# Loading two weight matrices by head, moving integer adds from GpSimd to VectorE, and reordering the first loads of a fused attention and feed-forward kernel

## The chip, the cores and the metric

The kernel runs on one core of a Trainium2 chip. The metric is device time in microseconds, from the median of several executions; lower is better. The engines named below are TensorE (PE in the profile; its weight loads are PEld), VectorE (DVE), ScalarE (ACT), GpSimd (POOL) and SyncE (SP), which issues all DMA transfers of this kernel. The core has 16 DMA engines.

## The reference

The inputs are q, k, v, a_re and a_im of shape (4, 8, 768, 48), that is batch, heads, time and width of a head, in float32. The weights w1 and w2 (384 x 1024), w3 (1024 x 1024) and w_out (1024 x 384) come in float64.

```python
mag = np.sqrt(a_re * a_re + a_im * a_im)
scale = np.minimum(mag, 0.999) / (mag + 1e-06)
a_re_n, a_im_n = (a_re * scale, a_im * scale)
for t in range(S):
    new_re = ar * S_re - ai * S_im          # ar, ai: row t of a_re_n, a_im_n
    new_im = ar * S_im + ai * S_re
    S_re, S_im = (new_re + k_t v_t^T, new_im)
    y[:, :, t] = q_t @ S_re
x = y.transpose(0, 2, 1, 3).reshape(B * S, H * D)
out = ((x @ w1) * (x @ w2)) @ w3 @ w_out
```

## The kernel before, in words

The host passes q, k and the gates with time last, v with the heads beside each other, and w3 transposed; the float64 weights are passed as they are.

The work is cut into eight units of 384 time steps, two to a batch. For each unit `gates(u)` computes the running product of the gates on ScalarE, VectorE and GpSimd (logarithm, exponential, arctangent, scans, sine) and scales q and k with it. `parts` splits its operations into three for unit 0 only. At its end copies from one place of the on-chip memory to another (line 563) lay the results out by head as KL and QL, and it requests unit u+2's gates. `scores` and `outputs` do the attention in three chunks of 128 steps. `ffn_ab` multiplies by w1 and w2 (line 636), and `ffn_out` by one matrix w3 @ w_out (line 646), which the kernel computes beforehand in `fuse` (line 713).

All weights are converted from float64 words to float32 in `convert`. A raw tile holds pairs of 32-bit words, 128 rows of up to 8 KB; three raw tiles rotate (pool `cv3`). ScalarE makes `low`, the rounded top bits of the low word (line 668), and `mag`, the square that finds tiny values (669). VectorE shifts and masks the high word (670, 672). An integer add puts `low` on it (673), and VectorE multiplies by the result of a comparison (674). `low` and `mag` have one buffer each, the converted tile two. There are 18 conversions: four of w_out (128 x 768 values each), eight of w3 and six of w1 and w2 (128 x 1024 each).

For w1 and w2 the rows are laid out as the attention delivers them: tile 0 holds the first 32 rows of heads 0 to 3, tile 1 those of heads 4 to 7, tile 2 the last 16 rows of all eight heads. Each tile is one transfer whose source has heads as its outermost dimension, then rows, then 8 KB of words.

The list `work` holds w_out's four conversions, then for each of eight columns of w3 a conversion and a `fuse`, then w1's and w2's six conversions. The main program calls them in turn and takes one step of unit 0's `gates` after each. Then the pools of the conversion are closed (line 760), and a pool `late` is opened in their place, which holds unit 1's q, k and results. After that a loop over the units mixes attention, feed-forward of the unit before, and steps of the next unit's gates.

A tile framework takes these calls as the order of precedence. A planner in it fixes, before the kernel runs, each engine's own order of instructions from dependencies, free buffers and its estimate of durations. On the chip every engine then works strictly in that order, SyncE's issues too. Each transfer waits on one of eight transfer semaphores that are used in turn, so at most eight transfers are on their way. A last branch computes everything in another way if the gates are out of bounds; it isn't taken with these inputs.

Of the kernel before, what the change touches and what calls it, by code (L numbers as in the profile page):

```python
# [10 lines left out]
FP = mybir.dt.float32  # L11
# [3 lines left out]
OP = mybir.AluOpType  # L15
# [300 lines left out]
def kernel(  # L316
# [37 lines left out]
    nc = tc.nc  # L354
    B, H, D, S = qt.shape
    P = 128
# [6 lines left out]
    KF = FF // P  # L363
# [3 lines left out]
    LO, HI = 32, D - 32  # L367
# [48 lines left out]
    def load_rows(dst, src, u):  # L416
        b, h = divmod(u, 2)
        for f in range(KD):
            nc.sync.dma_start(out=dst[:, f, 0:TT], in_=src[b, :, DG * f:DG * (f + 1), h * TT:(h + 1) * TT].rearrange(  # L419
                "h d s -> d h s"))  # L420

    def load_gates(u):
        g = g_t[u] = {}
        for n, src in (("re", art), ("im", ait)):
            g[n] = two.tile([P, KD, TT], FP, tag=n, name=n)
            load_rows(g[n], src, u)

    def load_qkv(u):
        b, h = divmod(u, 2)
        g = g_t[u]  # L430
        g["q"] = sides[u % 2].tile([P, KD, TT], FP, tag="q", name="q")
        g["k"] = sides[u % 2].tile([P, KD, TT + UC], FP, tag="k", name="k")
        load_rows(g["k"], kt, u)
        load_rows(g["q"], qt, u)

        vr = one.tile([P, UC, DM], FP, tag="vr", name="vr")
        nc.sync.dma_start(out=vr, in_=v[b, h * TT:(h + 1) * TT].rearrange("(c p) e -> p c e", p=C))
        g["vr"] = vr
# [217 lines left out]
    LOAD = 1024  # L656
    MIN_SQ = (1.125 * 2.0 ** -15) ** 2

    def convert(dst, src):
        r, m = dst.shape[1:]  # L660
        raw = cv3.tile([P, r, m, 2], I32, tag="raw", name="raw")
        nc.sync.dma_start(out=raw.rearrange("p r m w -> p r (m w)"), in_=src)
        lo, hi = raw[:, :, :, 0], raw[:, :, :, 1]
        low = cv1.tile([P, r, m], I32, tag="low", name="low")
        mag = cv1.tile([P, r, m], FP, tag="mag", name="mag")
        f = cv2.tile([P, r, m], FP, tag="cf", name="cf")
        b = f.bitcast(I32)
        nc.scalar.activation(out=low, in_=lo.bitcast(U32), func=AF.Copy, scale=2.0 ** -29)  # L668
        nc.scalar.activation(out=mag, in_=hi.bitcast(FP), func=AF.Square)
        nc.vector.tensor_scalar(out=b, in0=hi, scalar1=3, scalar2=0x3FFFFFFF, op0=OP.logical_shift_left,  # L670
                                op1=OP.bitwise_and)
        nc.vector.scalar_tensor_tensor(out=b, in0=hi, scalar=-0x40000000, in1=b, op0=OP.bitwise_and, op1=OP.bitwise_or)  # L672
        nc.gpsimd.tensor_tensor(out=b, in0=b, in1=low, op=OP.add)  # L673
        nc.vector.scalar_tensor_tensor(out=dst, in0=mag, scalar=MIN_SQ, in1=f, op0=OP.is_ge, op1=OP.mult)  # L674

    def load_weight(dst, src):
        if src.dtype == FP:
            nc.sync.dma_start(out=dst, in_=src)
        else:
            convert(dst, src)  # L680

    def words(src):
        return src if src.dtype == FP else src.bitcast(I32)

    def w12_work():

        got = []
        for d, w in ((w1s, w1), (w2s, w2)):
            hs = words(w).rearrange("(h e) m -> h e m", e=D)
            for f, src in enumerate((hs[0:4, 0:LO], hs[4:8, 0:LO], hs[:, LO:D])):  # L690
                got.append(lambda d=d, f=f, src=src: load_weight(d[:, f:f + 1], src))
        return got

    wo_s = one.tile([P, KF, DM], FP, tag="ab", name="wo_s")
    w3_t = {}

    def wo_work():
        src = words(wo).rearrange("(i p) m -> p i m", p=P)
        return [lambda i=i: load_weight(wo_s[:, i:i + 2], src[:, i:i + 2]) for i in range(0, KF, 2)]

    def w3_work(j):
        n = 1 if w3t.dtype == FP else 2
        src = words(w3t).rearrange("(i p) m -> p i m", p=P)[:, :, n * j * P:n * (j + 1) * P]

        def load():
            w3_t[j] = two.tile([P, KF, P], FP, tag="xT", name="w3s")
            load_weight(w3_t[j], src)
        return [load]

    def fuse(j):  # L710
# [34 lines left out]
    cv2 = conv.enter_context(tc.tile_pool(name="cv2", bufs=2))  # L745
    cv3 = conv.enter_context(tc.tile_pool(name="cv3", bufs=3))
    load_gates(0)
    load_qkv(0)
    work = wo_work()
    for j in range(KF):  # L750
        work += w3_work(j) + [lambda j=j: fuse(j)]
    work += w12_work()
    start = gates(0, True)
    load_gates(1)
    for i, f in enumerate(work):
        f()
        next(start, None)
    for _ in start:
        pass
    conv.close()  # L760
    sides[1] = fast.enter_context(tc.tile_pool(name="late", bufs=1))
    load_qkv(1)
# [63 lines left out]
```

## Time and profile before

| what | value |
|---|---|
| median of 3 runs | 746.97 us (745.07 to 749.74) |
| profiled execution | 749.98 us, span 748.2 us |
| TensorE busy | 587.1 us (78%) |
| VectorE busy | 354.0 us (47%) |
| ScalarE busy | 256.2 us (34%) |
| GpSimd busy | 147.9 us (20%) |
| moved by DMA | 65.76 MB, mean 88 GB/s |

Times in the profile are microseconds from the start of the span unless marked ns. A row of a group reads: line, engine, operation, output<-input, shapes, count, then busy time and mean ns of one, then the idle time before it and what ended it. A row of the waits reads: who <- for whom, total us, times, longest. A row of the timeline reads: start, length, engine, line, operation. "SPq" is SyncE's queue of issues. The DMA share is the mean busy share of the 16 DMA engines. TensorE's granted clock is given as a share of full speed.

### The profile page before, as it was taken

The numbers are of one execution on the slowest core, as the hardware profiler recorded it, in microseconds if no ns is written. First come the engines' busy times: TensorE is split into PE (matmuls) and PEld (weight loads), VectorE is DVE, ScalarE is ACT, GpSimd is POOL, SyncE is SP. The second block draws the span as 40 slices with busy tenths as digits, with TensorE's granted clock in tenths as the row PEclk, the third lists the DMA queues.
The fourth block names the chain that finished last, engine by engine and source line by source line (L and its number), as shares of the span: only waits on it lengthen the run. The fifth ranks groups of instructions, "written<-read, shape, count | busy, mean of one in ns | idle before, by whom it ended". The sixth has DMA issues, their size and how long they took to land.

```text
span 748.2 us, 8868 instructions
## 1 busy us (share of the span) xinstructions
PE 587.1 (78%) x3514; PEld 381.9 (51%) x3514; DVE 354.0 (47%) x491; ACT 256.2 (34%) x362; POOL 147.9 (20%) x131
## 2 busy tenths in 40 slices
PE   0028788038882489997998989999988998999997
PEld 0014465024451365674566646765675567567553
DVE  3889715334857457425811681178038713112110
ACT  6444531225464634315403540363046202100110
POOL 5474403414212141102101210131023000000000
PEclk9999998659997589999998999999989999999999
DMA  8755963452079670395301950097047005500001
GB/s 234 243 169 160 185 142 113 119 141 83 2 108 155 80 134 0 96 117 106 95 1 31 131 157 1 0 127 191 1 62 98 11 0 77 73 0 23 13 0 36
DMA packets 44563, 65.76 MB, mean 88 GB/s; under 512 B 3808, under 2 KB 42720, under 8 KB 43744
## 3 DMA queue, kind: packets, MB, share of 16 engines
q1 hardware_dynamic: 44512, 65.10, 43.5%
q8 instruction: 29, 0.48, 0.3%
q14 instruction: 22, 0.18, 0.1%
HBM read 41.42 MB, written 4.72 MB: 62 GB/s over the span
## 4 chain that ended last, share of the span: by engine, by line
PE 49%; DVE 20%; ACT 10%; DMA 8%; issue 7%; POOL 2%; SPq 2%; DVEq 0%; ACTq 0%; POOLq 0%
PE m L636 18%; PE o L646 16%; DMA raw<-in_w_dram 6%; PE sc L583 5%; DVE gZ L533 3%; PE kv L619 3%; DVE gA L508 3%; PE tp L578 2%; ACT gZ L469 2%; ACT gR L469 2%; POOL cf L673 2%; SPq L419 1%; PE f L713 1%; DVE cf L670 1%; ACT KT L579 1%
## 5 line engine op out<-in xcount | busy, mean ns | idle before, releaser
L636 PE MATMUL m<-xT,w1s 128*128 128x384 f32 x384 | 141.7, 506 | 20.6 <-ACT xT L614 12.7
L636 PE MATMUL m<-xT,w2s 128*128 128x384 f32 x384 | 136.0, 490 | 5.3 <-ACT a L640 2.9
L646 PE MATMUL o<-w3o,ab 128*128 128x384 f32 x384 | 129.5, 494 | 0.7 <-DVE ab L641 0.7
L636 PEld LDWEIGHTS m<-xT,w1s 128*128 128x128 f32 x384 | 73.4, 197 | 74.9 <-DVE ab L641 14.5
L636 PEld LDWEIGHTS m<-xT,w2s 128*128 128x128 f32 x384 | 73.0, 191 | 59.3 <-ACT a L640 6.0
L584 DVE COPY_PREDICATED A<-causal,sc 128x512 f32<-128x512 int32 x48 | 35.1, 738 | 140.3 <-PE sc L583 140.0
L646 PEld LDWEIGHTS o<-w3o,ab 128*128 128x128 f32 x384 | 72.5, 192 | 49.1 <-issue 2.1
L713 PE MATMUL f<-wo_s,w3s 128*128 128x384 f32 x128 | 50.3, 556 | 59.3 <-DVE w3s L674 59.3
L641 DVE TENSOR_TENSOR ab<-m,a 128x384 f32<-128x384 f32 x64 | 35.4, 552 | 96.1 <-PE m L636 93.1
L713 PEld LDWEIGHTS f<-wo_s,w3s 128*128 128x128 f32 x128 | 27.4, 218 | 81.4 <-DVE w3s L674 59.0
L640 ACT COPY a<-m 128x384 f32<-128x384 f32 x64 | 30.2, 474 | 110.3 <-PE m L636 110.2
L484 POOL TENSOR_TENSOR im<-im,gR 128x1152 f32<-128x1152 f32 (+1 forms) x10 | 20.7, 2075 | 199.4 <-ACT gR L469 194.7
L673 POOL TENSOR_TENSOR cf<-cf,low 128x1024 int32<-128x1024 int32 (+1 forms) x18 | 47.3, 2630 | 59.4 <-DVE cf L672 30.4
L583 PE MATMUL sc<-QL,KL 96*128 96x128 f32 x384 | 55.6, 309 | 0.0
L583 PEld LDWEIGHTS sc<-QL,KL 96*128 96x128 f32 x384 | 53.0, 221 | 3.0 <-issue 1.0
L579 ACT COPY KT<-tp 128x384 f32<-128x384 f32 x40 | 19.1, 478 | 99.5 <-PE tp L578 98.7
L668 ACT ACTIVATE low<-raw 128x1024 int32<-128x1024 uint32 (+1 forms) x18 | 19.8, 1102 | 80.5 <-POOL cf L673 42.5
L601 PE MATMUL y<-A,V 128*32 128x128 f32 x384 | 20.5, 285 | 26.4 <-ACT xT L614 26.4
L670 DVE TENSOR_SCALAR cf<-raw 128x1024 int32<-128x1024 int32 (+1 forms) x18 | 16.9, 942 | 40.2 <-DMA raw<-in_w_dram 33.8
L619 PEld LDWEIGHTS kv<-V,KT 128*96 128x96 f32 x320 | 30.7, 167 | 6.1 <-issue 4.4
L578 PE MATMUL tp<-ident,gR 128*128 128x128 f32 x60 | 12.3, 321 | 26.8 <-DVE gR L549 21.6
L614 ACT COPY xT<-y 128x384 f32<-128x384 f32 x24 | 11.3, 473 | 62.9 <-PE y L612 41.4
(88 smaller groups left out, 704.3 us busy)
## 6 DMA issues: line engine op xcount, KB each, us to landing
raw<-in_w_dram SPq DMA_DIRECT2D x14, 1024.0 KB, 5.5
KL<-gR SPq DMA_DIRECT2D x24, 193.5 KB, 6.1
KL<-k SPq DMA_DIRECT2D x24, 193.5 KB, 7.1
re<-in_a_re_dram SPq DMA_DIRECT2D x24, 192.0 KB, 9.1
im<-in_a_im_dram SPq DMA_DIRECT2D x24, 192.0 KB, 8.3
k<-in_k_dram SPq DMA_DIRECT2D x24, 192.0 KB, 6.1
q<-in_q_dram SPq DMA_DIRECT2D x24, 192.0 KB, 4.6
vr<-in_v_dram SPq DMA_DIRECT2D x8, 576.0 KB, 6.0
```

The costliest lines, as they stand in the source:

```text
L469: chain(nc.scalar.activation(**kw))
L578: nc.tensor.transpose(out=tp[:, f], in_=src[:, f, w], identity=ident)
L579: nc.scalar.copy(out=KT[:, :, x], in_=tp.rearrange("p f c -> p (f c)").rearrange("p (d h) -> p h d", h=H))
L583: nc.tensor.matmul(out=sc[:, j], lhsT=KL[:, hd, w], rhs=QL[:, hd, w], start=True, stop=True)
L584: nc.vector.copy_predicated(out=A[:, x * H // 2:(x + 1) * H // 2], data=sc, mask=causal.rearrange("p (h t) -> p h t", h=1).to_broadcast([P ...
L619: nc.tensor.matmul(out=kv[:, hd], lhsT=KT[:, hd], rhs=V[:, hd], start=True, stop=True)
L636: nc.tensor.matmul(out=m, lhsT=w[:, f, j * P:(j + 1) * P], rhs=xT_t[u][:, f], start=(f == 0), stop=(f == KD - 1))
L640: nc.scalar.copy(out=a, in_=got[0])
L641: nc.vector.tensor_tensor(out=ab_t[u][:, j], in0=got[1], in1=a, op=OP.mult)
L646: nc.tensor.matmul(out=m, lhsT=ab_t[u][:, f, t * P:(t + 1) * P], rhs=w3o[:, f], start=(f == 0), stop=(f == KF - 1))
L673: nc.gpsimd.tensor_tensor(out=b, in0=b, in1=low, op=OP.add)
L713: nc.tensor.matmul(out=m, lhsT=w3_t[j][:, f], rhs=wo_s[:, f], start=(f == 0), stop=(f == KF - 1))
```

## The change

Three things are changed. The transfers of w1 and w2 are issued by head, four of 32 rows or eight of 16 rows to a tile, each with rows as the outermost dimension of its source. The integer add of `convert` goes from GpSimd to VectorE, for all 18 conversions. And at the start, w_out's first two loads come ahead of the loads of unit 0's k, q and v; the loads of unit 1's gates come after the eleventh item of `work`; and the steps of unit 0's gates begin with the second item, not with the first.

```diff
-    def convert(dst, src):
+    def convert(dst, srcs):
         r, m = dst.shape[1:]
+        n = P // len(srcs)
         raw = cv3.tile([P, r, m, 2], I32, tag="raw", name="raw")
-        nc.sync.dma_start(out=raw.rearrange("p r m w -> p r (m w)"), in_=src)
+        for i, src in enumerate(srcs):
+            nc.sync.dma_start(out=raw[i * n:(i + 1) * n].rearrange("p r m w -> p r (m w)"), in_=src)
...
-        nc.gpsimd.tensor_tensor(out=b, in0=b, in1=low, op=OP.add)
+        nc.vector.tensor_tensor(out=b, in0=b, in1=low, op=OP.add)
...
         for d, w in ((w1s, w1), (w2s, w2)):
-            hs = words(w).rearrange("(h e) m -> h e m", e=D)
-            for f, src in enumerate((hs[0:4, 0:LO], hs[4:8, 0:LO], hs[:, LO:D])):
-                got.append(lambda d=d, f=f, src=src: load_weight(d[:, f:f + 1], src))
+            hs = words(w).rearrange("(h x e) m -> h e x m", x=1, e=D)
+            for f, (h0, h1, e0, e1) in enumerate(((0, 4, 0, LO), (4, 8, 0, LO), (0, H, LO, D))):
+                srcs = [hs[hd, e0:e1] for hd in range(h0, h1)]
+                got.append(lambda d=d, f=f, srcs=srcs: load_weight(d[:, f:f + 1], srcs))
...
     load_gates(0)
-    load_qkv(0)
+    start = gates(0, True)
     work = wo_work()
     for j in range(KF):
         work += w3_work(j) + [lambda j=j: fuse(j)]
     work += w12_work()
-    start = gates(0, True)
-    load_gates(1)
     for i, f in enumerate(work):
         f()
-        next(start, None)
-    for _ in start:
-        pass
+        if i == 1:
+            load_qkv(0)
+        if i == 10:
+            load_gates(1)
+        if i >= 1:
+            next(start, None)
     conv.close()
```

`load_weight` passes the list of sources on; w_out and w3 give it a list of one, so their transfers are as before.

More of the change, by code (lines that the diff above doesn't have):

```diff
@@ L672, in convert, with load_weight @@
         nc.vector.scalar_tensor_tensor(out=b, in0=hi, scalar=-0x40000000, in1=b, op0=OP.bitwise_and, op1=OP.bitwise_or)
-        nc.gpsimd.tensor_tensor(out=b, in0=b, in1=low, op=OP.add)
+        nc.vector.tensor_tensor(out=b, in0=b, in1=low, op=OP.add)
         nc.vector.scalar_tensor_tensor(out=dst, in0=mag, scalar=MIN_SQ, in1=f, op0=OP.is_ge, op1=OP.mult)
[L676 to L680, printed above, removed]
+    def load_weight(dst, srcs):
+        if srcs[0].dtype != FP:
+            return convert(dst, srcs)
+        n = P // len(srcs)
+        for i, src in enumerate(srcs):
+            nc.sync.dma_start(out=dst[i * n:(i + 1) * n], in_=src)
     def words(src):
@@ L698, in wo_work @@
         src = words(wo).rearrange("(i p) m -> p i m", p=P)
-        return [lambda i=i: load_weight(wo_s[:, i:i + 2], src[:, i:i + 2]) for i in range(0, KF, 2)]
+        return [lambda i=i: load_weight(wo_s[:, i:i + 2], [src[:, i:i + 2]]) for i in range(0, KF, 2)]
     def w3_work(j):
@@ L706, in load @@
             w3_t[j] = two.tile([P, KF, P], FP, tag="xT", name="w3s")
-            load_weight(w3_t[j], src)
+            load_weight(w3_t[j], [src])
         return [load]
```

## The prediction

> **What bounds the kernel now.** I first read the span and then busy time by stage. I chose the cuts where the timeline changes character: the start, w_out's conversions, w3's conversions, the first unit's attention, w1 and w2, and all the rest.
>
> ```profile
> span 748.2 us, 8868 instructions
> ...
> 0.00:22.00 22.00, 0.00 (x0) 0.00 (x0) 6.09 (x24) 12.20 (x27) 11.58 (x24) 1.00 0.90 252
> 22.00:50.00 28.00, 0.00 (x0) 0.00 (x0) 25.30 (x30) 14.99 (x21) 19.29 (x16) 1.00 0.65 215
> 50.00:94.00 44.00, 34.68 (x88) 18.99 (x89) 39.12 (x45) 20.84 (x27) 21.97 (x10) 0.92 0.72 160
> 94.00:116.00 22.00, 19.22 (x139) 14.70 (x141) 5.72 (x8) 5.77 (x10) 0.00 (x0) 1.00 0.54 132
> 116.00:178.00 62.00, 25.82 (x205) 15.95 (x196) 25.89 (x26) 16.14 (x18) 23.16 (x16) 0.67 0.43 113
> 178.00:748.20 570.20, 507.35 (x3092) 332.23 (x3092) 251.83 (x361) 186.24 (x259) 71.89 (x66) 0.95 0.39 65
> ```
>
> The columns are length, then busy time of TensorE, its weight loads, VectorE, ScalarE and GpSimd, then granted clock, DMA share and GB/s. From 178 us on TensorE is busy 507 of 570 us; nothing in the diff touches that stage. From 22 to 94 us VectorE is the full engine. From 116 to 178 us no engine is: VectorE 25.9 of 62 us, DMA share 0.43. The chain that ended last says what that stage waits for (start, length, what):
>
> ```profile
> 118.05 19.86 DMA raw<-in_w_dram
> ...
> 142.91 28.51 DMA raw<-in_w_dram
> ...
> 176.86 1.24 DVE w2s L674
> ...
> 178.12 1.17 ACT gA L469
> ```
>
> 48.4 us of the 62 are transfers of w1 and w2. When the last of w2 is converted (178.1 us), unit 1's gates start: their memory is that of the conversion's pools. So 178.1 us, which I call E, is the end of a prelude, and what E gains the whole kernel gains, unless the later stage changes. I read next why the transfers are slow, and VectorE's waits up to 180 us (total, times, longest):
>
> ```profile
> 132.00:142.00 10.00, 0.11 (x4) 0.00 (x0) 6.64 (x6) 4.09 (x5) 5.71 (x4) 0.76 0.25 105
> ...
> ACT low L668 <- POOL cf L673: 42.5, 12, 9.9
> DVE cf L670 <- DMA raw<-in_w_dram: 33.8, 5, 10.3
> ...
> DVE T L623 <- PE kv L619: 11.3, 1, 11.3
> ...
> DVE w3s L674 <- POOL cf L673: 7.6, 3, 3.0
> DVE gZ L489 <- ACT gZ L469: 7.0, 1, 7.0
> ...
> DVE cf L670 <- DMA raw<-in_w_out_dram: 6.4, 1, 6.4
> ```
>
> With only w1/w2 in flight the DMA share is 0.25: four of sixteen engines, at 105 GB/s. A megabyte takes 10 us. The source of such a load has four heads outermost.
>
> **The loads by head.** Pieces of 32 or 16 rows have rows outermost, and I take it that all 16 engines then work: 4 x 105 = 420 GB/s, 2.5 us for a megabyte. [...] On the other side stand issue and landing:
>
> ```profile
> re<-in_a_re_dram SPq DMA_DIRECT2D x3, 192.0 KB, 3.3
> ...
> 4.69 1.88 SPq L419 DMA_DIRECT2D k<-in_k_dram  x3
> ...
> 145.49 13.07 SPq L419 DMA_DIRECT2D q<-in_q_dram  x3
> ...
> SPq L662 <- DVE cf L672: 37.9, 6, 14.8
> ...
> q1 hardware_dynamic: 3410, 4.40, 105.6%
> ```
>
> An issue costs SyncE 0.63 us (1.88 / 3). Six transfers become 32, so 26 more issues, 16.4 us of SyncE. A four-piece load is 2.5 us of issue, an eight-piece one 5.0. SyncE has the time: it stood 37.9 us waiting for VectorE to free a raw buffer. Behind the pieces on SyncE wait only loads for units 1 and 2, which nothing reads before E. Three small loads issued 0.6 us apart land 3.3 us after issue each, so they overlap. I take 2.5 to 5.0 us a load, 20 us for all six (four at 2.5, two at 5.0). Now they cost about 50: four at 10 us, and two whose source has eight heads outermost, so by the same rate per engine 5 us each. The last row is all traffic from 76 to 100 us: the first unit's copies into KL and QL and unit 2's gates fill the engines. The change doesn't shorten that, and loads behind it land late.
>
> **The adds on VectorE.** Per conversion and by form (busy, mean ns):
>
> ```profile
> L672 DVE SCALAR_TENSOR_TENSOR cf<-raw,cf 128x1024 int32<-128x1024 int32 x14 | 17.2, 1232 | 0.1
> L670 DVE TENSOR_SCALAR cf<-raw 128x1024 int32<-128x1024 int32 x14 | 14.7, 1055 | 33.8 <-DMA raw<-in_w_dram 33.8
> L674 DVE SCALAR_TENSOR_TENSOR w3s<-mag,cf 128x1024 f32<-128x1024 f32 x8 | 9.7, 1216 | 7.6 <-POOL cf L673 7.6
> L508 DVE TENSOR_TENSOR_SCAN gA<-gA,gZ 128x128 f32<-128x128 f32 x9 | 8.2, 943 | 0.0
> L533 DVE TENSOR_TENSOR_SCAN gZ<-im 128x384 f32<-128x384 f32 x3 | 5.7, 1908 | 0.0
> ...
> L672 DVE SCALAR_TENSOR_TENSOR cf<-raw,cf 128x768 int32<-128x768 int32 x4 | 3.7, 932 | 0.0
> ...
> L540 DVE TENSOR_SCALAR re<-re 128x384 f32<-128x384 f32 x3 | 3.2, 1065 | 0.0
> ...
> L673 POOL TENSOR_TENSOR cf<-cf,low 128x1024 int32<-128x1024 int32 x14 | 38.8, 2770 | 49.1 <-ACT mag L669 27.7 <-DVE cf L672 20.1 <-DVE w3s L674 1.3
> ...
> L668 ACT ACTIVATE low<-raw 128x1024 int32<-128x1024 uint32 x14 | 16.2, 1155 | 67.8 <-POOL cf L673 36.7 <-DMA raw<-in_w_dram 31.2
> ```
>
> No integer add on VectorE is in the trace. The nearest rows are L672 and L674, same tile, two inputs: 1.22 to 1.23 us, 0.93 for w_out. I take 14 x 1.23 + 4 x 0.93 = 20.9 us. GpSimd loses 47 us of adds, which take 2.77 us each; ScalarE's 42.5 us of waiting for them goes, for `low` has one buffer.
>
> Against the 20.9 us stands what GpSimd does to VectorE. Timeline:
>
> ```profile
> 14.07 1.06 DVE L508 TENSOR_TENSOR_SCAN gA<-gA,gZ 128x128 f32<-128x128 f32 x3
> ...
> 60.49 5.43 PE L713 MATMUL f<-wo_s,w3s 128*128 128x384 f32 x16 [1.64 <-DVE w3s L674]
> 61.49 0.94 DVE L533 TENSOR_TENSOR_SCAN gZ<-im 128x384 f32<-128x384 f32 x1
> 61.71 2.86 POOL L673 TENSOR_TENSOR cf<-cf,low 128x1024 int32<-128x1024 int32 x1 [3.21 <-ACT mag L669]
> 62.36 2.77 DVE L670 TENSOR_SCALAR cf<-raw 128x1024 int32<-128x1024 int32 x1
> ...
> 70.82 0.35 DVE L540 TENSOR_SCALAR re<-re 128x384 f32<-128x384 f32 x1
> ...
> 72.10 0.68 DVE L670 TENSOR_SCALAR cf<-raw 128x1024 int32<-128x1024 int32 x1
> ```
>
> The L670 beside an add took 2.77 us, the one alone 0.68. Mean less undisturbed: L670 14 x 0.375 = 5.2, L508 9 x (0.943 - 0.353) = 5.3, L533 3 x 0.97 = 2.9, L540 3 x 0.72 = 2.1: 15.5 us. Bounds are 0 (the stretch is another GpSimd operation's) and 15.5; I take all of it, since those long instructions fall beside adds.
>
> The adds now stand in VectorE's order with a wait for ScalarE's `low`; behind them wait L674, the gates and the first unit's masked copies, and TensorE's fuse waits for L674. `low` (1.16 us) runs beside L670 and L672 (0.68 + 1.23), so the wait is nothing unless ScalarE is late with gate work: 0 to 18 x 1.2; I take 2.
>
> **The moves.** w_out's first two loads pass k, q and v (seven issues) and unit 1's gates (six issues), the last going behind the eleventh work item. This removes most of the 6.4 us wait; k, q and v land later by 1.57 MB at 252 GB/s, 6 us; w_out's conversions (4 x 3.4 us of VectorE) cover that, and without the cover it costs those 6 us. Unit 1's gates are read first at 178 us. The gate steps each come one work item later. I take nothing, between 0 and 6 us. w3's tile has two buffers, so its third conversion waits for the first fuse (5.43 us of matmul); VectorE needs 4.4 a conversion plus gates, so TensorE is close behind and would be the next bound.
>
> **The sum.** VectorE's busy time up to 178 us is 6.09 + 25.30 + 39.12 + 5.72 + 25.89 = 102.1, so it idles 76. After: 102.1 + 20.9 - 15.5 = 107.5. Idle after: waits for raw 40.2 fall to 8 (0 to 20, the loads behind KL and QL); the wait for kv 11.3 to 6 (0 to 11.3, it hangs on where the planner puts the first attention); for the add 7.6 to the 2 for `low`; L489's 7.0 stays; the 9.8 left becomes 7.5. Together 30.5. E becomes 138, 40 us earlier. The DMA share summed over the same stages is 108 us, so DMA doesn't forbid 138 but forbids much under 120. The profiled execution took 749.98 us (span 748.2 and 1.8 around it); the median shown is 746.97. So 710 against the profiled one, **707 us** against the median. The later stage I keep at 570 us, give or take 8 for another plan and a TensorE that starts less cold (0.67 granted from 116 to 178 us).
>
> **Rivals.** (1) *Everything fits better*: no kv or raw waits, E = 107.5 + 14.5 = 122, 691 us. For it: VectorE and DMA both allow it. Against: both are near full, and orders are fixed beforehand. (2) *VectorE becomes the bound*: no relief (123), raw waits 20, kv 11.3, the rest 14.5: E = 169, 738 us; with half the relief and the forecast's other waits 715. Long L670s beside L673 speak against. (3) *The loads stay on few engines*, so the change isn't what it says: then only the first stage gains. What w_out's first load passes is 12 issues of 192 KB and v's 576 KB, 2.95 MB at 252 GB/s, 12 us: 735 us. For it: only a source with few rows outermost is in the trace at this row length. Against: loads of 128 rows reach 252 GB/s in the first stage. (4) *Slower: SyncE's queue stalls on each piece.* The three q issues at 145 us took 13.07 us, 4.4 each, since SyncE waits for older transfers to land. If each piece is issued when the one ahead has landed, 3.3 us, then 32 pieces take 106 us where six loads take 50: E near 222 less the 12 gained before, 210, 779 us. It decides from 50 / 32 = 1.6 us a piece. The re loads speak against. [...]
>
> **Chances.** Forecast (694 to 722) 0.60, (1) 0.13, (2) 0.14, (3) 0.05, (4) 0.05, no change by several small losses 0.03. A measurement here can tell about 1%, 7.5 us. Faster by more 0.89, within 0.05, slower 0.06. The range 688 to 733 takes in most of (1) and half of (2).
>
> **What would show it.** DMA share above 0.8 while w1/w2 load, each piece landing 3 to 5 us after issue; L670 near 0.7 us beside no add; an add near 1.23 us; the last L674 near 138 us; the stage after it 570 us. Wrong if raw waits stay at 30 us and more, VectorE's total to E passes 120, or the later stage grows.

## The result, and the profile after

The changed kernel takes 708.98 us (median of 4 runs, 704.26 to 713.92), beside 748.36 us for the kernel before on the same chip: a ratio of 0.948, 95% interval 0.940 to 0.956. The profiled execution of it took 713.92 us, span 712.1. Runs more than 1.5% above the fastest of the same kernel that were measured with them are left out of the gains and ratios below.

The last weight tile is finished at 144.8 us, where it was 178.1, so I cut the span there; the other cuts are those of the prediction, moved along. Columns as before: length, busy time of TensorE, its weight loads, VectorE, ScalarE, GpSimd, granted clock, DMA share, GB/s.

```profile
0.00:22.00 22.00, 0.00 (x0) 0.00 (x0) 8.38 (x21) 12.89 (x25) 8.15 (x14) 1.00 0.91 252
22.00:50.00 28.00, 11.80 (x29) 6.73 (x30) 27.96 (x44) 20.33 (x29) 12.29 (x12) 1.00 0.91 275
50.00:87.50 37.50, 31.21 (x106) 18.54 (x105) 36.54 (x52) 19.77 (x29) 13.44 (x13) 0.91 0.85 188
87.50:110.00 22.50, 20.41 (x218) 16.14 (x220) 7.31 (x12) 2.77 (x6) 1.58 (x6) 1.00 0.69 147
110.00:144.80 34.80, 16.18 (x86) 7.64 (x79) 26.20 (x25) 14.54 (x16) 2.10 (x3) 0.71 0.68 142
144.80:712.10 567.30, 509.47 (x3086) 333.82 (x3086) 251.97 (x360) 186.09 (x259) 71.92 (x66) 0.94 0.39 66
```

The stage of w1 and w2, 62 us before, takes 34.8, with VectorE busy 26.2 of them (25.9 before): the adds have come to it, and its waits for raw words of w1 and w2 are gone. w3's stage is 37.5 us in place of 44. The later stage is 567.3 us in place of 570.2. From 87.5 to 110 us VectorE still stands, busy 7.3 of 22.5 us, while TensorE does the first unit's attention. The chain that ended last, up to the first step of unit 1's gates (start, length, what):

```profile
115.06 4.18 DMA raw<-in_w_dram
...
123.99 6.89 DMA raw<-in_w_dram
130.90 5.30 DMA q<-in_q_dram
136.50 1.11 ACT low L670
...
143.52 1.24 DVE w2s L676
144.78 1.17 ACT gA L469
```

Of 48.4 us of transfers of w1 and w2 in the chain, 11.1 are left. The chain goes by the semaphore that came last, and the step through "DMA q" to `low` at 136.5 us misleads. From the timeline of ScalarE and VectorE:

```profile
130.62 0.69 DVE L672 TENSOR_SCALAR cf<-raw 128x1024 int32<-128x1024 int32 x1
...
136.09 0.48 ACT L640 COPY a<-m 128x384 f32<-128x384 f32 x1 [6.95 <-PE m L636]
136.46 1.14 ACT L670 ACTIVATE low<-raw 128x1024 int32<-128x1024 uint32 x1
...
137.64 1.23 DVE L675 CUSTOM_DVE_ANT_0 cf<-cf,low 128x2048 uint16<-128x2048 uint16 x1 [5.07 <-ACT low L670]
```

VectorE read the raw tile of this conversion at 130.6 us, so it had landed. `low` stood on ScalarE behind the copy of the first unit's product with w1 (L640), which had waited 6.95 us for TensorE. So the last long wait before E is one for ScalarE's order, not for a load.

VectorE's waits up to that point (total, times, longest):

```profile
DVE cf L672 <- DMA raw<-in_w_out_dram: 12.5, 2, 11.7
DVE T L625 <- PE kv L619: 9.8, 1, 9.8
DVE cf L675 <- ACT low L670: 7.3, 3, 5.1
DVE A L584 <- PE sc L583: 4.2, 6, 1.9
```

And its operations up to 150 us, by form (busy, mean ns):

```profile
L675 DVE CUSTOM_DVE_ANT_0 cf<-cf,low 128x2048 uint16<-128x2048 uint16 x14 | 17.1, 1220 | 7.7 <-ACT low L670 7.3
L672 DVE TENSOR_SCALAR cf<-raw 128x1024 int32<-128x1024 int32 x14 | 10.2, 730 | 0.0
L675 DVE CUSTOM_DVE_ANT_0 cf<-cf,low 128x1536 uint16<-128x1536 uint16 x4 | 4.6, 1150 | 0.1
L533 DVE TENSOR_TENSOR_SCAN gZ<-im 128x384 f32<-128x384 f32 x3 | 4.5, 1485 | 0.0
L508 DVE TENSOR_TENSOR_SCAN gA<-gA,gZ 128x128 f32<-128x128 f32 x9 | 3.6, 430 | 0.0
L540 DVE TENSOR_SCALAR re<-re 128x384 f32<-128x384 f32 x3 | 1.1, 409 | 0.0
```

L675 is the add that was GpSimd's (L673 before; two lines were added above). L672 is the shift, 1055 ns before, and L508 the scan, 943 ns before.

### The profile page after: what moved, and what is told of

Its sections match the earlier page's. It is cut to its first block, busy times and chain, and to the rows that moved or that the text cites. A ratio compares the mean times of both kernels' runs of the same rounds, so it can differ in the third digit from the quotient of the medians.

```text
span 712.1 us, 8939 instructions
## 1 busy us (share of the span) xinstructions
PE 589.1 (83%) x3514; PEld 382.9 (54%) x3514; DVE 358.4 (50%) x509; ACT 256.4 (36%) x362; POOL 109.5 (15%) x113
## 4 chain that ended last, share of the span: by engine, by line
PE 55%; DVE 20%; ACT 10%; issue 8%; DMA 4%; SPq 2%; DVEq 0%; ACTq 0%
PE m L636 19%; PE o L646 16%; PE sc L583 7%; PE f L718 4%; PE kv L619 3%; DVE gZ L533 3%; DVE gA L508 2%; PE tp L578 2%; ACT gR L469 2%; ACT gZ L469 2%; DMA q<-in_q_dram 2%; DMA raw<-in_w_dram 2%; DVE cf L675 2%; PE y L601 2%; ACT KT L579 2%
## 5 line engine op out<-in xcount | busy, mean ns | idle before, releaser
L636 PE MATMUL m<-xT,w1s 128*128 128x384 f32 x384 | 143.9, 511 | 17.4 <-DVE w1s L676 10.0
L636 PE MATMUL m<-xT,w2s 128*128 128x384 f32 x384 | 138.2, 496 | 9.8 <-DVE w2s L676 8.6
L718 PE MATMUL f<-wo_s,w3s 128*128 128x384 f32 x128 | 47.9, 538 | 42.9 <-DVE w3s L676 42.9
L640 ACT COPY a<-m 128x384 f32<-128x384 f32 x64 | 30.3, 474 | 121.2 <-PE m L636 119.6
L583 PE MATMUL sc<-QL,KL 96*128 96x128 f32 x384 | 57.6, 317 | 0.0
L583 PEld LDWEIGHTS sc<-QL,KL 96*128 96x128 f32 x384 | 55.0, 229 | 2.9 <-issue 0.8
L520 POOL TENSOR_TENSOR q<-q,gA 128x1152 f32<-128x1152 f32 (+1 forms) x10 | 28.5, 2847 | 61.4 <-DVE gA L508 48.5
L619 PE MATMUL kv<-V,KT 128*96 128x64 f32 x320 | 30.8, 248 | 0.9 <-DVE T L625 0.9
L670 ACT ACTIVATE low<-raw 128x1024 int32<-128x1024 uint32 (+1 forms) x18 | 19.7, 1095 | 22.5 <-DVE cf L675 18.4
L521 POOL TENSOR_TENSOR k<-k,gR 128x1152 f32<-128x1152 f32 (+1 forms) x10 | 23.3, 2341 | 23.5 <-DVE gR L518 23.5
```

Of the source, the lines that this page charges most:

```text
L520: nc.gpsimd.tensor_tensor(out=q[:, s], in0=q[:, s], in1=A[:, s], op=OP.mult)
L583: nc.tensor.matmul(out=sc[:, j], lhsT=KL[:, hd, w], rhs=QL[:, hd, w], start=True, stop=True)
L619: nc.tensor.matmul(out=kv[:, hd], lhsT=KT[:, hd], rhs=V[:, hd], start=True, stop=True)
L636: nc.tensor.matmul(out=m, lhsT=w[:, f, j * P:(j + 1) * P], rhs=xT_t[u][:, f], start=(f == 0), stop=(f == KD - 1))
L640: nc.scalar.copy(out=a, in_=got[0])
L718: nc.tensor.matmul(out=m, lhsT=w3_t[j][:, f], rhs=wo_s[:, f], start=(f == 0), stop=(f == KF - 1))
```

## The experiments

Each line of this table is a kernel; "gain" is its median against that of the kernel before, measured beside it, E the end of the last conversion in its profiled execution, "rest" the span after E. The parts one at a time, the pairs and the change were measured apart from each other, so rows of different groups are compared by their ratios. (In the expectations single letters also name theories; in this text E is only that time.)

| kernel | gain, us | ratio, 95% interval | E, us | rest, us |
|---|---|---|---|---|
| before | | | 178.1 | 570.1 |
| loads alone | 4.3 | 0.992 (0.988 to 0.996) | 172.8 | 568.4 |
| adds alone | 2.1 | 0.995 (0.991 to 0.999) | 170.3 | 572.4 |
| order alone | -6.6 | 1.009 (1.005 to 1.013) | 185.4 | 569.6 |
| loads and adds | 31.0 | 0.960 (0.953 to 0.967) | 148.7 | 568.2 |
| adds and order | 11.7 | 0.989 (0.981 to 0.996) | 160.1 | 564.7 |
| loads and order | 10.3 | 0.988 (0.984 to 0.992) | 166.8 | 568.9 |
| the change | 39.4 | 0.948 (0.940 to 0.956) | 144.8 | 567.3 |

### One part at a time

**Loads alone**: the changed kernel with add and order as before.

```diff
-        nc.vector.tensor_tensor(out=b, in0=b, in1=low, op=OP.add)
+        nc.gpsimd.tensor_tensor(out=b, in0=b, in1=low, op=OP.add)
...
-    start = gates(0, True)
+    load_qkv(0)
     work = wo_work()
...
+    start = gates(0, True)
+    load_gates(1)
...
-        if i == 1:
-            load_qkv(0)
-        if i == 10:
-            load_gates(1)
-        if i >= 1:
-            next(start, None)
+        next(start, None)
+    for _ in start:
+        pass
```

> The kernel before with the transfers of w1 and w2 by head alone; adds on GpSimd, loads in the old order. Theory A (the transfers of w1 and w2 were the larger part of what the prelude lost): the prelude ends at 145 to 158 us instead of 178, the time is 715 to 728 us, and the two long DMA pieces of the chain shrink from 48 us to under 20. Rival B (the relief of VectorE from GpSimd's adds carries the gain): 738 us or more, and the waits for raw stay above 25 us because the conversions can't take the rows faster.

It took 741.58 us (735.23 to 743.02) beside 745.87, with E at 172.8: theory A falls. Rival B gave the time, but not the wait that it gave as the reason. The waits up to 175 us, all engines:

```profile
ACT low L670 <- POOL cf L675: 38.1, 13, 6.2
POOL cf L675 <- DVE cf L674: 37.5, 11, 7.3
```

No wait of VectorE for w1's and w2's raw words stands among VectorE's. In its place stands the loop through GpSimd: the add waits for VectorE's mask, and the next `low` waits for the add, for `low` has one buffer.

**Adds alone**: the kernel before with the add on VectorE.

```diff
-        nc.gpsimd.tensor_tensor(out=b, in0=b, in1=low, op=OP.add)
+        nc.vector.tensor_tensor(out=b, in0=b, in1=low, op=OP.add)
```

> The kernel before with the integer adds on VectorE alone; transfers and order as before. Theory A: the conversions of w_out and w3 end some 10 us earlier, but w1 and w2 still come over four and eight engines (10 and 5 us a load), so the prelude ends at 165 to 175 us and the time is 735 to 745 us. Rival B: 725 us or less. In both the mean of L670 falls from 1055 to 700 to 750 ns and VectorE's busy time up to the prelude's end is 105 to 110 us.

743.80 us (735.80 to 746.15) beside 745.87, with E at 170.3, as theory A said. The mean of the shift L670 is 744 ns and VectorE's busy time up to E 107.1 us, so the relief comes with the adds alone. VectorE's waits up to 172 us, and the chain:

```profile
DVE cf L670 <- DMA raw<-in_w_dram: 40.1, 5, 11.5
```

```profile
87.67 40.33 DMA raw<-in_w_dram
136.29 26.92 DMA raw<-in_w_dram
```

The waits for the raw words even grow (33.8 before), and the chain is the loads: conversions that are ready earlier wait longer for them.

**Order alone**: the kernel before with the new beginning.

```diff
-    load_qkv(0)
+    start = gates(0, True)
     work = wo_work()
...
-    start = gates(0, True)
-    load_gates(1)
     for i, f in enumerate(work):
         f()
-        next(start, None)
-    for _ in start:
-        pass
+        if i == 1:
+            load_qkv(0)
+        if i == 10:
+            load_gates(1)
+        if i >= 1:
+            next(start, None)
```

> The kernel before with the new order of the first loads alone. Theory A: w_out's first load lands 9 us earlier, at 13 us instead of 22, but the conversions behind it go at the pace of the adds on GpSimd and the end at the pace of w1's and w2's loads: 738 to 750 us. Rival C (the order alone moves the whole prelude up): 9 us less, 738 us or under.

752.48 us (748.62 to 759.29) beside 745.87: a small loss, with E 7 us later, above what either theory gave. Its chain:

```profile
115.46 29.34 DMA raw<-in_w_dram
149.86 28.43 DMA vr<-in_v_dram
```

Two long stretches of transfers stand in it as before, 57.8 us in place of 48.4, at the end with a load of v in the chain's row. What of the 7 us each moved load makes was not tried.

### Two parts at a time

The change, with one of its parts undone in each kernel; the three edits are those above.

Order undone (loads and adds):

> The changed kernel with the loads in the old order (transfers by head and adds on VectorE). Theory F (the conversions of w1 and w2 need a transfer, then the add, one after another, each fast enough alone to hide the other's gain; speeding up both is what pays): the prelude ends at 148 to 160 us, the time is 718 to 732 us, well under the sum of the two alone (5 and 3 us). Rival G (the gain of the whole hangs on the new order, the pair gains no more than its parts): 738 us or more.

711.04 us (709.53 to 718.72) beside 742.02, with E at 148.7. Loads and adds together bring 31.0 us, where singly they bring 4.3 and 2.1. The time is below theory F's range, so rival G falls: the pair's gain doesn't hang on the order.

Loads undone (adds and order):

> The changed kernel with w1 and w2 in six transfers as before (adds on VectorE, new order). Theory F: held by the transfers, some 57 us for the six behind KL and QL, so the prelude ends at 158 to 172 us and the time is 728 to 744 us, waits for raw 30 us or more. Rival G: 722 us or less.

730.28 us (726.62 to 734.38), in theory F's range. VectorE waits 29.4 us for w3's, w1's and w2's words, and the loads are the chain again:

```profile
85.95 34.71 DMA raw<-in_w_dram
126.06 27.50 DMA raw<-in_w_dram
```

Adds undone (loads and order):

> The changed kernel with the adds on GpSimd (transfers by head, new order). Theory F: held by the adds, a conversion of w1 or w2 every 5.6 us or longer, so the prelude ends at 165 to 178 us and the time is 733 to 748 us. Rival G: 722 us or less.

731.73 us (729.11 to 737.44), just below theory F's range, with E inside it (166.8). The waits up to 170 us:

```profile
POOL cf L675 <- DVE cf L674: 50.0, 9, 22.7
ACT low L670 <- POOL cf L675: 22.9, 9, 3.2
...
POOL cf L675 <- ACT low L670: 12.6, 2, 8.0
...
POOL cf L675 <- ACT xT L614: 11.8, 1, 11.8
```

GpSimd's loop is only a part of this. Where nothing else comes between, its adds of w1 and w2 start 5.6 us apart (128.96, 134.56 and 140.16 us), where VectorE's adds in "loads and adds" start 4.55 us apart (121.12 and 125.67). The last two rows are ScalarE's order: `low` stood behind copies that waited for TensorE.

So two limits of nearly the same height stand beside each other, the transfers with heads outermost and the add on GpSimd. Taking one away shows the other; only both together move E far. In all these kernels the rest after E is 565 to 572 us, so most of the difference in time is that in E. What the order is worth depends on its company: alone it puts E 7.3 us later, beside the adds 10.2 us earlier, beside the loads 6.0, beside both 3.9. By time only the loss of the order alone is clear of noise; the other pairs of intervals overlap.

### What a load by head costs

A kernel without the computation, which writes zeros, makes each kind of transfer twice with nothing else in flight (the first kind, four heads outermost, ran while the zeros were being written, so it isn't used). Each moves 128 rows of 8 KB:

```diff
+    def eight_heads():
+        nc.sync.dma_start(out=raw, in_=heads[:, 32:D])
...
+    def pieces_of_32():
+        for h in range(4):
+            nc.sync.dma_start(out=raw[32 * h:32 * h + 32], in_=heads[h, 0:32])
...
+    def pieces_of_16():
+        for h in range(8):
+            nc.sync.dma_start(out=raw[16 * h:16 * h + 16], in_=heads[h, 32:D])
...
+    def rows_128():
+        nc.sync.dma_start(out=raw, in_=w[0:P])
...
+    def rows_64():
+        for h in range(2):
+            nc.sync.dma_start(out=raw[64 * h:64 * h + 64], in_=w[64 * h:64 * h + 64])
...
+    def spread_32():
+        for h in range(4):
+            nc.sync.dma_start(out=raw[h:P:4], in_=heads[h, 0:32])
```

> Leaves out the whole computation: it writes zeros and then transfers 128 rows of 8 KB of w1 in nine ways, each twice, each way waiting for the one before. Theory D (a transfer's rate hangs on which partitions it writes): four pieces of 32 rows take about 4.8 us of transfer, 220 GB/s, and eight of 16 rows about 8 us, 131 GB/s, as in the changed kernel; one transfer of 128 rows 2.8 to 3.3 us; 32 rows written to every fourth partition as fast as 128 rows; two pieces of 64 consecutive rows no faster than pieces of 32. Rival E (each piece has a fixed cost that adds up): pieces to every fourth partition take the same 4.8 us as pieces to 32 neighbours, and pieces of 64 rows lie half way to one of 128. Four heads outermost: 10 us on a share of 0.25, eight heads 5 us on a share of 0.5.

VectorE's next operation waited, from issue to landing: 11.90 and 10.14 us for eight heads outermost, 6.91 and 6.92 for four pieces of 32 rows, 10.62 and 10.35 for eight pieces of 16, 4.91 and 4.89 for one of 128, 7.23 and 7.20 for two of 64, 6.19 and 6.02 for the pieces spread over every fourth partition. The pieces of 32 in another order took 6.76 and 6.58, and on two queues 7.38 and 6.62. One transfer of each kind, from its first packet to its last (length, VectorE, GpSimd, clock, DMA share, GB/s): eight heads outermost, pieces of 32, pieces of 16, one of 128, two of 64, 32 spread.

```profile
57.40:65.50 8.10, 0.00 (x0) 0.00 (x0) 1.00 0.45 128
74.70:79.75 5.05, 0.00 (x0) 0.00 (x0) 1.00 0.92 208
92.90:100.65 7.75, 0.00 (x0) 0.00 (x0) 1.00 0.97 135
108.90:112.40 3.50, 0.00 (x0) 0.00 (x0) 1.00 0.81 297
114.45:119.45 5.00, 0.00 (x0) 0.00 (x0) 1.00 0.93 210
136.05:140.35 4.30, 0.00 (x0) 0.00 (x0) 1.00 0.72 244
```

The DMA engines are busy for 0.72 to 0.97 of the time in all but the first, and yet the rate is 135 to 297 GB/s. By these rows (length x share x 16 engines, over 128 packets) a packet of 8 KB takes 0.35 us with 128 rows, 0.39 with 32 spread ones, 0.58 with 32 or 64 neighbouring partitions, 0.94 with 16. Two pieces of 64 neighbouring partitions are no faster than four of 32 (5.00 and 5.05 us), though there are half as many, and four spread over every fourth partition take 4.30. So theory D holds in the main for these transfers, that the rate hangs on which partitions are being written at one time, and a fixed cost of each piece, its rival, isn't what slows the neighbouring pieces. Why a packet to neighbouring partitions takes longer is not shown. A piece has some cost of its own, though: the spread pieces, whose packets are nearly as fast as those of the one large transfer (0.39 and 0.35 us), take 4.3 us in place of 3.5, and theory D had them equal.

### Loads over 128 partitions

The change, with the rows of w1 and w2 copied by the host into the order of the tiles, so that each tile is one transfer of 128 rows (six issues in place of 32).

```diff
-        for d, w in ((w1s, w1), (w2s, w2)):
-            hs = words(w).rearrange("(h x e) m -> h e x m", x=1, e=D)
-            for f, (h0, h1, e0, e1) in enumerate(((0, 4, 0, LO), (4, 8, 0, LO), (0, H, LO, D))):
-                srcs = [hs[hd, e0:e1] for hd in range(h0, h1)]
+        for d, w, wx in ((w1s, w1, w1x), (w2s, w2, w2x)):
+            for f, (s, g) in enumerate(((w, 0), (w, 1), (wx, 0))):
+                srcs = [words(s).rearrange("(i p) m -> p i m", p=P)[:, g:g + 1]]
...
-        "w1": moe_w1,
+        "w1": moe_w1.reshape(H, D, -1)[:, :32].reshape(H * 32, -1),
+        "w1x": moe_w1.reshape(H, D, -1)[:, 32:].reshape(H * (D - 32), -1),
```

(and the same for w2)

> The changed kernel with the rows of w1 and w2 laid out by the host in the order of the tiles (a copy, like the host's other layouts), so that each tile is one transfer of 128 rows that writes all partitions. A tile's transfer takes 3.4 us where the pieces take 4.9 or 7.7, so six take 20 us where they take 35. Theory H (in the changed kernel the transfers still hold up the last conversions): the prelude ends 4 to 9 us earlier, 700 to 706 us. Rival I (the planner's order holds them up: VectorE stands before the first unit's attention from 88 to 110 us and ScalarE's low behind a copy that waits for TensorE): less than 3 us.

695.33 us (694.25 to 698.56) beside 742.02: ratio 0.939 (0.932 to 0.946). E is 133.0, the rest 563.7. Against "loads and adds" on the same chip, 709.53 to 718.72, which has the old order too, it is faster in every run. Against the change E is 11.8 us earlier, more than either theory gave; by the ratios, whose intervals overlap, the gain in time isn't certain. Its stage of w1 and w2, same columns as at the top:

```profile
110.00:133.00 23.00, 4.54 (x106) 3.40 (x96) 23.00 (x25) 12.07 (x11) 3.77 (x5) 0.60 0.57 184
```

VectorE is busy all 23 us. That this comes from the shorter transfers is not shown. In the change neither VectorE (up to E) nor ScalarE (from 100 us on) waits for words of w1 or w2, so the transfers weren't what they stood for there. And the layout also changed the planner's order: the copy of the first unit's product with w1, which stood ahead of `low` at 126.6 and 136.1 us in the change, first comes at 138.9 us here, behind all conversions, and w1's first conversion starts at 106.0 us in place of 110.5. Rival I's cause, the order, was thus changed along with the loads; the two were not tried apart. The copying by the host is not in the device's time.

### Where w1 and w2 stand in the list

Two orders were tried to fill VectorE's stand from 88 to 110 us, each with the loads by head and with the host's layout. First, w1's and w2's conversions between w3's columns:

```diff
+    w12 = w12_work()
     for j in range(KF):
         work += w3_work(j) + [lambda j=j: fuse(j)]
-    work += w12_work()
+        if 1 <= j <= 6:
+            work.append(w12[j - 1])
```

> The kernel after the change, with the conversions of w1 and w2 put between w3's column tiles in the planner's list, so that they are planned ahead of the first unit's attention. Theory F (VectorE stood from 88 to 110 us after the change because the attention of the first unit was planned ahead of w1's conversions, and its softmax waits on TensorE): the last conversion of w2 comes at 118 to 132 us instead of 144.7, the rest of the span stays at 564 to 572 us, and the time is 688 to 700 us against 709. Rival G (that time was work which has to be done somewhere: the attention only moves behind the conversions, and the first unit's chain starts as late): the last conversion comes earlier, but the rest of the span grows by as much, and the time stays at 705 to 713 us.

726.57 us (723.68 to 729.47) beside 747.38: ratio 0.973 (0.965 to 0.982), slower than the change. E is 162.2, the rest 565.5. Neither theory foretold that. (There is no softmax in this attention; in the change VectorE waits there for kv and the scores, 9.8 and 4.2 us.) Unit 1's gates start at 173.9 us in this order, behind the last fused product, so E isn't the end of the prelude here. VectorE's waits up to 165 us, and ScalarE's from 85 to 165 us:

```profile
DVE cf L675 <- ACT low L670: 33.1, 5, 8.1
```

```profile
ACT w3o L719 <- PE f L718: 54.5, 4, 21.0
```

And the chain shows the round:

```profile
127.40 1.24 DVE w3s L676
128.68 7.96 PE f L718 x16
137.04 1.14 ACT low L670
138.20 1.24 DVE cf L675
```

`low` of a w2 tile stands on ScalarE behind the copy of a fused column (L719), which waits 8 us for TensorE (7.96 in the chain), and VectorE waits for `low` before it can convert the next column for TensorE.

> The same order of conversions, with the rows of w1 and w2 laid out in the order of the tile by the host, so that each tile comes in one transfer over 128 partitions. Theory F: the loads of w1 and w2 and the stand of VectorE are two separate costs; the last conversion comes at 110 to 122 us, the rest stays at 564 to 570 us, and the time is 678 to 690 us, under the 695 us of the layout alone by 5 or more. Rival G: as the layout alone, 692 to 698 us.

690.68 us (688.46 to 697.99) beside 747.38: ratio 0.930 (0.920 to 0.939), E 124.4, rest 562.3. It falls just above the range of the one theory and below that of the other. This is the fastest of all; its interval lies just below that of the change, but overlaps with the layout alone (0.932 to 0.946), so these two can't be told apart. In its trace ScalarE waits little for the fused columns:

```profile
ACT w3o L720 <- PE f L719: 7.4, 4, 4.7
```

Why the planner put ScalarE's work in a better order with this layout was not tried.

Second, w1 and w2 ahead of all of w3:

```diff
+    work += w12_work()
     for j in range(KF):
         work += w3_work(j) + [lambda j=j: fuse(j)]
-    work += w12_work()
```

> The kernel after the change, with the six conversions of w1 and w2 planned straight behind those of w_out and ahead of all of w3's. Theory H (the version with w1 and w2 between w3's columns was slow, 726.6 us, because ScalarE runs in order: its low for a w1 or w2 tile stood behind the copy of a fused column, and the copy behind 7 to 8 us of TensorE, in turn waiting for the column that VectorE had just converted): with the six together no conversion of w1 or w2 stands behind a fused column; the waits of VectorE for ScalarE's low fall from 33.1 us to under 12, the last conversion comes at 130 to 146 us, and the time is 694 to 710 us. Rival I (it was slow because the loads by head, at half the rate, then stand ahead of w3's and delay the fused product; eight fused columns of 7 to 8 us each follow the loads wherever the order puts them): the fused product starts 30 us or more later, the last conversion comes at 152 us or later, and the time is 715 to 735 us.

710.08 us (706.98 to 712.91) beside 745.71: ratio 0.952 (0.944 to 0.961), E 142.0, rest 569.1, which can't be told from the change. VectorE's waits for `low` up to 150 us are 3.7 us in place of 33.1, and the time went from 726.6 to 710.1, just past the upper edge of what the theory of the standing queue gave:

```profile
DVE cf L675 <- ACT low L670: 3.7, 1, 3.7
```

The first fused product came at 85.8 us, 48 us later than in the change (38.2), as the rival said. Its matmuls now stand in the chain right ahead of the last conversion:

```profile
122.65 18.07 PE f L718 x48
```

So this order trades one bound for another, and E comes out 2.8 us ahead of the change's.

> The same order, w1 and w2 ahead of w3, with the rows of w1 and w2 laid out in the order of the tile by the host, so that each of their tiles comes in one transfer over 128 partitions. Theory H: the loads are no part of the matter, so the time is that of the layout with w1 and w2 last, 690 to 700 us, or a little under. Rival I: six loads of 5 us in place of six of 5 to 8 us take 12 to 18 us off the version with the loads by head, and what is left, the fused product behind six conversions, keeps the time at 700 to 718 us, slower than the layout with w1 and w2 last (695.3).

701.16 us (696.63 to 704.49) beside 745.71: ratio 0.941 (0.932 to 0.950), E 129.3, rest 570.3. It falls 1.2 us above the one theory's range and inside the other's; by its interval it can't be told from the layout with w1 and w2 last. In its trace, too, 48 matmuls of the fused product, 17.2 us, begin at 121.1 us, and they outlast E. What the two orders show together is that VectorE's stand was not 22 us for the taking: with the loads by head, neither order was faster than the change.

## Why the prediction came out right, point by point

**The end of the prelude sets the time: right.** E went from 178.1 to 144.8 (forecast 138) and the later stage from 570.2 to 567.3 (forecast 570). The two deviations, +6.8 and -2.9, make 713.9 of the forecast 710 for a profiled execution. The median of the runs shown was 5 us lower still, so the nearness of 709 to 707 is partly luck.

**VectorE's busy time: right.** 106.4 us up to E, forecast 107.5. The adds took 17.1 + 4.6 = 21.7 us (forecast 20.9); w_out's took 1.15 us each, not 0.93. The relief, against the 15.5 us taken: L672 14 x (1.055 - 0.730) = 4.6, the scans L508 9 x 0.513 = 4.6, L533 3 x 0.42 = 1.3, L540 3 x 0.66 = 2.0, together 12.5. The busy time fell by 17.4 without the adds (102.1 + 21.7 - 106.4); the rest lies in rows that I hadn't counted: L549, for instance, went from 1253 to 544 ns.

**The idle time: sum near, terms wrong.** 38.4 us, forecast 30.5. Waits for raw words were to fall from 40.2 to 8: those of w3, w1 and w2 are gone from VectorE's list, but w_out's, which was to go nearly, is 12.5. L489's 7.0, which was to stay, is gone instead. These two belong together, 13.4 us before and 12.5 now: w_out's first conversion starts at 13.2 us in place of 22.0, and the gates, which filled that time before, come behind it. The wait for kv is 9.8 in place of 6, and `low` 7.3 in place of 2, inside the bounds given; its 5.07 and 1.41 us are the waits behind the copy L640, which the prediction had not looked at. That the errors in both directions left 8 us is luck in part. I treated these terms as if each stood for itself. The table shows that they don't: a sum of idle times says how much is to be had if all its causes go, and the three parts singly give 4.3 + 2.1 - 6.6 = -0.2 us of the 39.4.

**The load by head: the term that was mis-sized.** I took 420 GB/s, 2.5 us for a megabyte, from 4 x 105 GB/s and the assumption that sixteen engines would work. No run shows that rate. The engines do work, at a share of 0.92 and 0.97, but pieces of 32 neighbouring partitions move 208 GB/s and those of 16 135 GB/s in the transfers above; even one of 128 rows moves 297. In a transfer by itself four pieces take 6.9 us from issue to landing and eight 10.4, against 2.5 to 5.0. In the change the DMA share is 0.68 over that stage; from 117 to 122 us, with pieces on their way, it reads 1.02, so the sign of a share above 0.8 came without the rate (221 GB/s, with all other traffic). And a piece lands 7.3 us (32 rows) or 6.9 us (16 rows) after its issue, not 3 to 5. The profile's list of issues up to 160 us (count, KB each, median us to landing):

```profile
raw<-in_w_dram SPq DMA_DIRECT2D x16, 256.0 KB, 7.3
...
raw<-in_w_dram SPq DMA_DIRECT2D x16, 128.0 KB, 6.9
```

Before, too, I was off: eight heads outermost take 10 to 12 us by themselves, at a share of 0.45, not the 5 that I estimated. VectorE waited for none of these words in the change: three raw buffers let the loads run from 83.6 us on, beside w3's conversions and the first attention. So it isn't shown that the mistake cost anything; with the layout over 128 partitions E is 11.8 us earlier, but the planner's order differs there too.

**Issue on SyncE: on the safe side.** The issue of a load of raw words took 0.31 to 0.52 us, 0.37 in the median, against 0.63 taken from strided gate loads. The 32 pieces, with their waits, ran from 83.6 to 126.3 us:

```profile
83.62 42.68 SPq L664 DMA_DIRECT2D raw<-in_w_dram  x32
```

That is 1.3 us a piece, but not because each waits for the one ahead to land. SyncE's waits in that stretch:

```profile
SPq L664 <- DVE cf L674: 16.9, 3, 12.4
SPq L664 <- DMA raw<-in_w_dram: 7.7, 9, 1.0
```

More than half of the waiting is for VectorE to free a raw buffer. Rival (4), the queue that stalls on each piece, falls: its waits for older pieces are 7.7 us in all. Four pieces of 32 rows don't reach the rate of one transfer of 128, though (208 against 297 GB/s).

**The moves: nothing, as forecast, but for both signs.** Alone they lose 6.6 us; in company the difference from 711.0 to 709.0 us, measured apart, can't be told from nothing.

**Rivals.** (3) falls: sixteen engines work on the pieces, at a share of 0.92 and 0.97 where they are alone. (2) falls: the relief came. (1) falls for the change, whose E is 144.8, not 122; the kernels with the host's layout come near it, 695 and 691 us where it said 691.

## What to carry to other kernels

When the chain shows one wait, look for the second that stands beside it at nearly the same height: here the loads and the add were worth 4 and 2 us singly and 31 together, so a change that brings nothing alone may be half of one that does. A busy DMA share is not a rate (0.97 went with 135 GB/s here, 0.81 with 297): read the GB/s beside it, and ask which partitions the transfers write. And before filling an engine's stand by reordering, look at what the moved work queues behind on the other engines; that queue can stand before the move, too, as the copy ahead of `low` does here.

## What the hardware showed that I had not expected

A megabyte came at a different rate by the partitions that its transfers wrote: 297 GB/s at 128 rows, 208 to 210 in pieces of 32 or 64 neighbouring ones, 135 in pieces of 16, all at a DMA share of 0.81 to 0.97. VectorE's integer add appears as a custom operation on pairs of 16-bit words and yet takes 1.22 us, like the other two-input operations on this tile (1.27 for L674, 1.21 to 1.23 for L676), where GpSimd took 2.77. And taking GpSimd's adds away shortened VectorE's single-input shift from 1055 to 730 ns on average (744 with the adds alone).
